# The first half of every expert placed alongside a 12-chunk recurrence, with the experts' weights in quarter slices

## The chip, the cores and the metric

One core of a Trainium2 chip. Its engines run side by side, each through its own list of instructions in order: PE (TensorE) does matmuls, in which one operand is loaded as weights and the other streams through; DVE (VectorE), ACT (ScalarE) and POOL (GpSimd) do elementwise work; SP only starts transfers, one after the other, and a transfer that has to wait holds up those behind it. The metric is the device time of one execution in microseconds (us), lower is better.

## What is computed

The reference, cut to what matters. A recurrence over 768 steps for 4 x 8 heads with a 40 x 40 state each, and then a mixture of eight experts of which every token takes one.

```python
for t in range(S):                                   # 768 steps, state (4, 8, 40, 40)
    y[:, :, t] = np.einsum('bhd,bhde->bhe', rt, state)
    Sa = np.einsum('bhde,bhe->bhd', state, at)
    state_decay = state * wt[:, :, None, :] - np.einsum('bhd,bhe->bhde', Sa, bt)
    state = state_decay + np.einsum('bhd,bhe->bhde', vt, kt)
...
logits = x @ w_gate                                  # x: the 3072 tokens of y, 320 wide
e_idx = np.argmax(logits, axis=1)
for e in range(E):                                   # 8 experts, w1 320 x 1024, w2 1024 x 320
    h = np.maximum(x[mask] @ w1[e], 0.0)
    out[mask] = gate_w[mask, None] * eom[mask, e, None] * (h @ w2[e])
```

All inputs and outputs are float32.

## The kernel before, in words

**The recurrence** (class `Att`) is cut into 12 chunks `c` of 64 steps, and each chunk into two halves of 8 head pairs, `q` = 0 and 1; I call one (c, q) a half chunk, and there are 24. A chunk needs three things. `prep` scales the inputs and builds small triangular matrices: matmuls `pl` (L241) and transposes `pt` (L159), with the running products of `scan` (L118). `tinv` inverts 32 x 32 triangles on DVE (L276 to L317, tiles `tmpf`, `Tt`, `Yt`), for a batch of two chunks at a time, and brings the result through DRAM into the tile `Tc` (L325, two buffers). `crit` is the serial part of a half chunk: a matmul into the PSUM tile `pa` (L370, two buffers), a solve (L380), a correction (L407), a second solve (L380), each with a copy by ACT in between, and the state of the next chunk by `pS` (L427) and two DVE operations (L432, L433). `tail` makes the output of the half chunk: transposes `ptU` and `ptS` (L449, L456), `pM` (L463), `pY` (L480, L481), and the DVE product `x` (L483), which is thus done once per half chunk. After most steps of `crit` and `tail` a few matmuls with zero weights are issued that compute nothing (`fill`, `warm`, L128, tile `fl`).

**The routing.** `route` writes `x` to DRAM, transposes it (`pxt`, L635) and computes its logits (L642). `pick` then ranks the tokens of a batch of chunks: matmuls of one-hot rows (L679 to L687), some twenty small DVE operations on the tile `mem`, and scatters into a table `tab` in DRAM (L714), in which each expert owns 480 slots. The batches (`NB`) come after chunks 3, 7, 10 and 11. After chunk 7 (`HALF`) the next free slot of every expert is moved to at least 240, so that the first two of its four tiles of 120 slots hold tokens of chunks 0 to 7 alone and can be worked on from then.

**The experts** (class `Moe`). A float32 number is split into a high part and a rest, and a product is the sum of three matmuls. `weights` loads all of an expert's w1 and w2 into staging tiles `st` (L738 to L748), lets ACT round a copy (`w1h`, `w2h`) and DVE subtract it (`w1l`, `w2l`, L744, L750). `tokens` gathers the rows of its tiles (`xg`, L764), transposes them (`px`, L772) and splits them (`xh`, `xl`, L774, L775). `expert` goes over eight blocks of 128 hidden units: eight matmuls into `ph` (L794, as many columns as there are slots: 240 for two tiles, 480 for four), of which the last has 64 rows of weights, then `hh` by ACT and `hl` by DVE (L798, L799). I call these eight a hidden block. Then, per tile of 120 slots, 24 matmuls into `po` (L807 to L809), a scaling (L811) and a scatter to the output (L812).

**The order of the work.** `run` (L500 on) interleaves by hand: after each step of `crit` a step of the previous `tail`, four steps (`RATE`) of a background list, and one of the routing. The background is `prep` and `tinv` of all chunks in turn, and then `early`: weights of expert 0, its first two tiles, and five (`E0`) of its hidden blocks. `need(c + 1)` runs the background until the inverses of the next chunk are emitted. When the chunks are done, `experts` does the rest, unit by unit: experts 0 and 1 in two halves, 2 to 7 with all four tiles. A scheduler of the language then sorts the list of each engine by its own estimate of time, so what stands in the lists is read below from the built programs.

Of the kernel before, what the change touches and what calls it, by code (L numbers as in the profile page):

```python
# [21 lines left out]
NP = 16  # L22
FAST = 1
DSC = 4
RATE = 4

# [27 lines left out]
class Att:  # L54
# [3 lines left out]
    def __init__(s, ctx, tc, ident, win, din, rl, vl, vt, nch=12):  # L58
# [23 lines left out]
        s.Tt = s.cp.tile([128, 1056], F32, name="Tt")  # L82
# [12 lines left out]
        s.fl = s.ps.tile([128, 512], F32, name="fl", tag="fl")  # L95
        s.buffers()
        s.st, s.ld, s.post, s.idle, s.NsOf = {}, {}, [], False, {}
# [32 lines left out]
    def fill(s, step, x):  # L130


        s.warm(x, s.FILL[step])
# [127 lines left out]
    def tinv(s, cs):  # L261
# [97 lines left out]
    def crit(s, c, q):  # L359
# [7 lines left out]
        pa = s.ps.tile([128, 8, 40], F32, name="pa", tag="pa", bufs=2)  # L367
# [130 lines left out]
    def run(s, sink, then=None):  # L498
# [5 lines left out]
        ready = {}  # L504

        def preps(b):
            for c in b:
                yield from s.prep(c)
                if c + 1 < n:
                    s.scan(c + 1)  # L510

        def inv(b):
            yield from s.tinv(b)
            for c in b:
                ready[c] = True
# [18 lines left out]
        def need(c):  # L534
            while c not in ready:
                next(bg)
        need(0)
# [11 lines left out]
        for c in range(n):  # L549
            need(min(c + 1, n - 1))  # L550
            for q in range(2):
                for i, _ in enumerate(s.crit(c, q)):
# [8 lines left out]
                    adv(RATE)  # L561
# [13 lines left out]
E0 = 5  # L575


class Moe:
    def __init__(s, ctx, tc, ident, wg, wo, w1, w2, out):
# [22 lines left out]
        nc.vector.tensor_scalar(out=s.bnd, in0=iw, scalar1=float(CAP), scalar2=float(TS * s.HT), op0=ALU.mult, op1=ALU.add)  # L602
# [21 lines left out]
    HALF, HT, half = 7, 2, False  # L624
    NB = {3: (0, 4), 7: (4, 4), 10: (8, 3), 11: (11, 1)}
# [101 lines left out]
    def weights(s, e, wp, sp):  # L727

        nc = s.nc
        w1h = wp.tile([128, 3, FF], F32R, name="w1h", tag="w1h")  # L730
        w1l = wp.tile([128, 2, FF], F32R, name="w1l", tag="w1l")
        w2h = wp.tile([128, 8, DM], F32R, name="w2h", tag="w2h")
        w2l = wp.tile([128, 8, DM], F32R, name="w2l", tag="w2l")
        yield w1h, w1l, w2h, w2l
        for k in range(3):
            st = sp.tile([128, FF], F32, name="st", tag="st")
            if k < 2:
                nc.sync.dma_start(out=st, in_=s.w1[e, 128 * k:128 * k + 128])  # L738
            else:
                for h in range(2):  # L740
                    nc.sync.dma_start(out=st[64 * h:64 * h + 64], in_=s.w1[e, 256:320])
            nc.scalar.copy(out=w1h[:, k], in_=st)
            l, r = (w1l[:, k], slice(0, 128)) if k < 2 else (w1h[64:128, 2], slice(64, 128))
            nc.vector.tensor_tensor(out=l, in0=st[r], in1=w1h[r, k].bitcast(F32), op=ALU.subtract)  # L744
            yield
        for k, n in ((0, 3), (3, 3), (6, 2)):
            st = sp.tile([128, FF], F32, name="st", tag="st")[:, 0:n * DM].rearrange("p (k f) -> p k f", k=n)
            nc.sync.dma_start(out=st, in_=s.w2[e, 128 * k:128 * (k + n)].rearrange("(k p) f -> p k f", p=128))  # L748
            nc.scalar.copy(out=w2h[:, k:k + n], in_=st)
            nc.vector.tensor_tensor(out=w2l[:, k:k + n], in0=st, in1=w2h[:, k:k + n].bitcast(F32), op=ALU.subtract)  # L750
            yield

    def tokens(s, tabs, e, t0, nt, pool, psx):

        nc = s.nc
        m = 2 if pool is s.tp0 else 4
        rows = 256 * (s.HALF + 1) if t0 + nt <= s.HT else NTOK
        xh = pool.tile([128, 3, TS * m], F32R, name="xh", tag="xh")[:, :, 0:TS * nt]
        xl = pool.tile([128, 3, TS * m], F32R, name="xl", tag="xl")[:, :, 0:TS * nt]
        xg = pool.tile([TS, m, DM], F32, name="xg", tag="xg")  # L760
        tb, ti = (x[:, :, 4 * e + t0:4 * e + t0 + nt] for x in tabs)
        yield tb, ti, xh, xl
        for t in range(nt):
            nc.gpsimd.indirect_dma_start(out=xg[:, t], out_offset=None, in_=s.xd[0:rows],  # L764
                                         in_offset=bass.IndirectOffsetOnAxis(ap=ti[:, 0, t:t + 1], axis=0),
                                         bounds_check=rows - 1, oob_is_err=True)
        yield
        for k in range(3):
            n = 128 if k < 2 else 64
            pt = psx(TS * nt)  # L770
            for t in range(nt):
                nc.tensor.transpose(out=pt[0:n, TS * t:TS * t + TS], in_=xg[:, t, 128 * k:128 * k + n],  # L772
                                    identity=s.ident[0:TS, 0:TS])
            nc.scalar.copy(out=xh[0:n, k], in_=pt[0:n])  # L774
            nc.vector.tensor_tensor(out=xl[0:n, k], in0=pt[0:n], in1=xh[0:n, k].bitcast(F32), op=ALU.subtract)  # L775
            if k == 2:
# [297 lines left out]
```

## Time and profile before

| what | us |
|---|---|
| median of 3 runs (lowest, highest) | 951.22 (943.26, 955.48) |
| the profiled execution: its own time | 950.18 |
| its span, which the profile covers | 948.5 |
| first `x` of the recurrence | 128.50 |
| `x` of half chunks 18 and 24 (the last) | 521.39 and 662.28 |
| last matmul of the experts | 932.79 |

In the profile a row of a timeline gives the start, the length, the engine, the line, the operation, output and inputs, and in brackets how long the engine had been idle and what ended the wait. The length of a matmul is modelled and overlaps that of the next, so what a matmul costs in a stream is read from the distance between two starts. PEclk is the granted clock of PE, 1.00 being full speed. A row of a windows table gives the busy time of every engine in a stretch, its PEclk, the busy share of the transfer engines and the bytes moved. In the profile's records a float32 matmul is two entries (`pM x8` is four matmuls); those of the experts are one entry each.

### The profile page before, as it was taken

How to read it: one execution, taken by the hardware profiler on the slowest of the kernel's cores; microseconds unless marked ns; L12 is line 12 of the kernel's file. 1: busy time of each engine (PE TensorE's matmuls, PEld its weight loads, DVE VectorE, ACT ScalarE, POOL GpSimd, SP SyncE). 2: the span in 40 equal slices, each digit the busy share in tenths (PEclk: the TensorE clock that was granted, in tenths of full speed). 3: DMA queues.
4: the chain of work that ended last, by engine and by line, in shares of the span. 5: the costliest groups of instructions: out<-in, count | busy, mean ns of one | idle time of the engine just before them, and what ended most of it. 6: DMA issues, size and time to landing. Idle time of an engine off the chain costs nothing.

```text
span 948.5 us, 22268 instructions
## 1 busy us (share of the span) xinstructions
PE 864.7 (91%) x9226; PEld 720.2 (76%) x9226; DVE 508.5 (54%) x1040; ACT 352.0 (37%) x835; POOL 324.4 (34%) x520
## 2 busy tenths in 40 slices
PE   6569699899999999999994999999899999999993
PEld 5457478788788788887873788888788788788873
DVE  8656948957944882388872321112535553544320
ACT  2566354754356135635211311111324542433110
POOL 7445567576255534502012000002252412231001
PEclk9555759999599669999876565556699999999997
DMA  8965277476266427535334321000655634351000
GB/s 187 187 124 116 60 164 157 99 178 136 74 145 131 100 77 177 109 81 125 80 81 73 86 49 35 24 24 13 162 146 157 180 116 119 87 162 55 11 14 23
DMA packets 151749, 97.77 MB, mean 103 GB/s; under 512 B 122678, under 2 KB 136825, under 8 KB 151642
## 3 DMA queue, kind: packets, MB, share of 16 engines
q1 hardware_dynamic: 146922, 87.30, 39.6%
q0 software_dynamic: 3840, 8.91, 3.3%
q8 instruction: 74, 1.21, 0.5%
q14 instruction: 33, 0.27, 0.1%
q10 hardware_dynamic: 880, 0.08, 0.1%
HBM read 73.48 MB, written 18.26 MB: 97 GB/s over the span
## 4 chain that ended last, share of the span: by engine, by line
PE 64%; DVE 14%; issue 8%; DMA 7%; POOL 3%; ACT 1%; SPq 0%; POOLq 0%; ACTq 0%; DVEq 0%
PE ph L794 14%; PE fl L128 7%; DVE tmpf L309 6%; PE pM L463 5%; PE po L809 5%; PE po L807 4%; PE po L808 4%; PE pa L380 3%; PE pl L241 3%; PE pa L370 2%; PE pS L427 2%; PE pY L481 2%; PE pxt L642 2%; PE pY L480 2%; DMA Nd<-N 2%
## 5 line engine op out<-in xcount | busy, mean ns | idle before, releaser
L247 POOL TENSOR_SCALAR_AFFINE_SELECT LA<-LA 64x192 f32<-64x192 f32 x144 | 62.4, 458 | 107.2 <-ACT LA L245 106.6
L714 POOL DMA_INDIRECT tab<-rec,si x24 | 25.1, 1045 | 211.7 <-DVE rec L711 174.3
L799 DVE SCALAR_TENSOR_TENSOR hl<-ph,hh 128x480 fp32r<-128x480 f32 (+1 forms) x75 | 41.8, 565 | 89.0 <-ACT hh L798 88.9
L794 PE MATMUL ph<-xl,w1h 128*128 128x480 f32 (+3 forms) x225 | 86.0, 383 | 0.0
L812 POOL DMA_INDIRECT out_dram<-y,ti x32 | 34.4, 1074 | 150.3 <-DVE y L811 90.3
L241 PE MATMUL pl<-Am,KBt 120*128 120x192 f32 (+1 forms) x288 | 71.7, 398 | 15.1 <-ACT Am L234 12.4
L794 PE MATMUL ph<-xh,w1h 128*128 128x480 f32 (+1 forms) x225 | 82.0, 366 | 0.6 <-DVE mem L692 0.3
L807 PE MATMUL po<-w2h,hh 128*120 128x320 f32 x256 | 80.2, 317 | 0.0
L808 PE MATMUL po<-w2l,hh 128*120 128x320 f32 x256 | 78.9, 312 | 0.0
L809 PE MATMUL po<-w2h,hl 128*120 128x320 f32 x256 | 78.4, 323 | 0.0
L798 ACT ACTIVATE hh<-ph 128x480 fp32r<-128x480 f32 (+1 forms) x75 | 36.6, 498 | 109.4 <-PE ph L794 109.4
L241 PEld LDWEIGHTS pl<-Am,KBt 120*128 120x128 f32 x288 | 57.0, 241 | 20.7 <-ACT Am L234 13.0
L463 PE MATMUL pM<-R,VU 104*128 104x128 f32 x384 | 71.4, 346 | 0.0
L118 POOL TENSOR_TENSOR Q<-Q,w 120x96 f32<-120x96 f32 x112 | 66.7, 634 | 0.1
L463 PEld LDWEIGHTS pM<-R,VU 104*128 104x128 f32 x384 | 61.7, 245 | 5.8 <-issue 2.3
L380 PE MATMUL pa<-As,Tc 32*32 32x40 f32 x1664 | 58.9, 224 | 6.2 <-ACT Tc L328 3.4
L469 DVE TENSOR_TENSOR M<-pM,mM 128x512 f32<-128x512 f32 x34 | 23.4, 689 | 74.6 <-PE pM L463 74.4
L481 PE MATMUL pY<-KB,M 128*64 128x40 f32 x768 | 62.1, 253 | 1.5 <-DVE M L469 1.2
L380 PEld LDWEIGHTS pa<-As,Tc 32*32 32x32 f32 x1664 | 46.7, 127 | 19.7 <-issue 7.0
L480 PE MATMUL pY<-Sd,R 104*64 104x40 f32 x704 | 60.2, 253 | 1.5 <-DVE M L469 1.5
L481 PEld LDWEIGHTS pY<-KB,M 128*64 128x64 f32 x768 | 54.5, 163 | 6.7 <-issue 4.0
L128 PE MATMUL fl<-As,zb 128*32 128x128 f32 x288 | 59.1, 338 | 0.0
(195 smaller groups left out, 1969.1 us busy)
## 6 DMA issues: line engine op xcount, KB each, us to landing
D<-in_din_dram SPq DMA_DIRECT2D x24, 540.0 KB
st<-in_w_dram SPq DMA_DIRECT2D x16, 512.0 KB
st<-in_w_dram SPq DMA_DIRECT2D x16, 480.0 KB
XS<-in_vt_dram SPq DMA_DIRECT2D x24, 256.0 KB
XU<-in_vt_dram SPq DMA_DIRECT2D x24, 256.0 KB
Nd<-N SPq DMA_DIRECT2D x24, 256.0 KB
VU<-in_vl_dram SPq DMA_DIRECT2D x24, 208.0 KB
w<-in_win_dram SPq DMA_DIRECT2D x12, 360.0 KB
```

The costliest lines, as they stand in the source:

```text
L118: g.tensor_tensor(out=run(m, z), in0=run(m - 1, z), in1=wr(m, z), op=ALU.mult)
L128: s.nc.tensor.matmul(s.fl[0:32, 0:src.free_size()], s.zb[0:src.partition_size()], src, start=True, stop=True)
L241: nc.tensor.matmul(pl[:, i, 0:nj], KBt[:, g0 + i].rearrange("p n t -> p (n t)"), Am[:, 0:nj, g0 + i], start=True, stop=True)
L247: g.affine_select(out=la[:, :, i], in_=la[:, :, i], pattern=[[0, nj], [1, C]], base=0, channel_multiplier=-1, compare_op=ALU.is_gt, fill=0.0)
L380: nc.tensor.matmul(pa[o:o + 32, i], Tc[o:o + 32, p, :], x[o:o + 32, i, :], start=True, stop=True, tile_position=(o, o))
L463: nc.tensor.matmul(pM[:, i], VU[:, h0 + i].rearrange("p n t -> p (n t)"), R[:, :, h0 + i], start=True, stop=True)
L480: nc.tensor.matmul(o, R[:, side, i, :], Sd[:, i, :], start=True, stop=False)
L481: nc.tensor.matmul(o, Ms[i // 4][:, i % 4, side, :], KB[:, side, p, :], start=not c, stop=True)
L794: nc.tensor.matmul(ph, l, r, start=(i == 0), stop=(i == 7))
L807: nc.tensor.matmul(po, hh[f][:, ts_], w2h[:, f], start=(f == 0), stop=False)
L808: nc.tensor.matmul(po, hh[f][:, ts_], w2l[:, f], start=False, stop=False)
L809: nc.tensor.matmul(po, hl[f][:, ts_], w2h[:, f], start=False, stop=(f == 7))
```

## The change

- All eight experts are split in two halves. `early` now holds the first two tiles of all of them (`E0 = 8`), `experts` the last two of all of them. Every expert's weights are thus loaded and split twice.
- The weights come in slices of 256 hidden units (`FS`): `load` brings one slice of w1 (three transfers) and of w2 (one), `split1` and `split2` make high part and rest. `walk` runs over slices and emits in turn a hidden block, then the second matmuls of the block before it for both tiles (`second`, six matmuls of 320 columns; I call it a second block), then half of the next slice's split. Slices are loaded two ahead in `early` (two raw buffers) and five ahead in `experts` (six).
- The last matmul of a hidden block now has all 128 rows: the rest of `xl` is set to zero (L795).
- `early` waits six background steps (`LATE`) between gathering the first tokens and transposing them. Sixteen of its steps on, `hush` ends all fills, and from there two background steps (`RATE2`) are taken per step of `crit`, not four.
- `HALF` is chunk 6, and the routing batches come after chunks 3, 6, 8, 9, 10 and 11.
- `crit` of a chunk asks for the chunk's own inverses and for the `prep` of the next, no longer for the inverses of the next; `Tc` has three buffers. `pa` has one buffer instead of two, and the bank of `fl` is shared with `po`, which `early` uses with two buffers. `Tt` moves to a pool that is freed after the last inverse.

The core of the diff (`slots` is only moved, `tokens` becomes `fetch` and `turn`, `expert` becomes `hidden` and `second`):

```diff
-            Tc = s.st[c]["Tc"] = s.p2.tile([128, NP, 32], F32, name="Tc")
+            Tc = s.st[c]["Tc"] = s.p2.tile([128, NP, 32], F32, name="Tc", bufs=3)
...
-        pa = s.ps.tile([128, 8, 40], F32, name="pa", tag="pa", bufs=2)
+        pa = s.ps.tile([128, 8, 40], F32, name="pa", tag="pa")
...
-            need(min(c + 1, n - 1))
+            need('t', c)
+            need('p', min(c + 1, n - 1))
...
-                    adv(RATE)
+                    adv(RATE2 if s.quiet else RATE)
...
-E0 = 5
+E0 = 8
+HT = 2
+FS = 256
+LATE = 6
...
-    HALF, HT, half = 7, 2, False
-    NB = {3: (0, 4), 7: (4, 4), 10: (8, 3), 11: (11, 1)}
+    HALF, half = 6, False
+    NB = {3: (0, 4), 6: (4, 3), 8: (7, 2), 9: (9, 1), 10: (10, 1), 11: (11, 1)}
...
+    def load(s, e, g, p):
+        fs = slice(FS * g, FS * g + FS)
+        r1 = p.tile([128, 3, FS], F32, name="r1", tag="r1")
+        r2 = p.tile([128, 2, DM], F32, name="r2", tag="r2")
+        nc.sync.dma_start(out=r1[:, 0:2], in_=s.w1[e, 0:256, fs].rearrange("(k p) f -> p k f", p=128))
+        for h in range(2):
+            nc.sync.dma_start(out=r1[64 * h:64 * h + 64, 2], in_=s.w1[e, 256:320, fs])
+        nc.sync.dma_start(out=r2, in_=s.w2[e, fs].rearrange("(k p) f -> p k f", p=128))
...
-            seq += [(w1h[:, 2, fs], xh[:, 2]), (w1h[0:64, 2, fs], xl[0:64, 2])]
+        seq += [(w1h[:, 2, fs], xh[:, 2]), (w1h[:, 2, fs], xl[:, 2])]
...
+    def walk(s, units, tabs, first, raw, ahead, wp, tp, hp, psx, ps1, ps2, m):
...
+        for k, u in enumerate(units):
...
+            for g in range(4):
+                i = 4 * k + g
+                if more and g == 0:
+                    xg = s.fetch(tabs, tp, m, *units[k + 1])
+                if more and g == 2:
+                    nt = s.turn(xg, units[k + 1][2], tp, m, psx)
+                    Tn = next(nt)
+                for fi in range(2):
+                    h = s.hidden(W[i], T, fi, hp, TS * m, ps1)
+                    yield
+                    if pend:
+                        s.second(*pend, hp, ps2)
+                        yield
+                    pend = W[i], u, tabs, 2 * g + fi, h
+                    if i + 1 < len(sl):
+                        split(i + 1, fi)
+                    next(nt, None)
+                load(i + 1 + ahead)
...
+        w = s.walk([(e, 0, 2) for e in range(E0)], tabs, W, raw, 2, wp, tp, hp, psx, psx, ps2, 2)
+        for _ in range(LATE + 10):
+            yield next(w)
+        quiet()
+        yield from w
...
+        units = [(e, 0, 4) for e in range(E0, E)]
+        for e in range(E0):
+            units.insert(2 * e + 1 if e < E - E0 else len(units), (e, HT, 2))
```

How it moves the lists of the engines is shown at two places. The first is PE in chunk 10, around the transposes `ptS` and the correction (`pa<-As2,NT`) of one half chunk. Before:

```order
L427 MATMUL pS_6979<-XU2_162,KB_4242 40x40 x8
L380 MATMUL pa_6992<-As_7011,Tc_4945 32x40 x13
L642 MATMUL pxt_6951<-G_70,xT_6955 128x16 x3
L380 MATMUL pa_6992<-As_7011,Tc_4945 32x40 x3
L128 MATMUL fl_146<-As_7011,zb_144 32x128 x2
L370 MATMUL pa_7193<-XS1_157,LA_4993 64x40
L456 MATMUL ptS_7045<-ident_58,XS2_161 128x40 x8
L128 MATMUL fl_146<-VU0_148,zb_144 32x128
L370 MATMUL pa_7193<-XS1_157,LA_4993 64x40 x4
L463 MATMUL pM_7055<-R0_147,VU0_148 128x128 x4
L407 MATMUL pa_6992<-As2_7043,NT_4245 32x40 x16
L128 MATMUL fl_146<-As2_7043,zb_144 32x128 x2
```

Now, at the same place:

```order
L461 MATMUL ptS_7510<-ident_58,XS2_161 128x40 x8
L412 MATMUL pa_7413<-As2_7508,NT_4780 32x40 x7
L468 MATMUL pM_7520<-R0_147,VU0_148 128x128 x4
L412 MATMUL pa_7413<-As2_7508,NT_4780 32x40 x9
L840 MATMUL po_7592<-w2h_7449,hh_7475 120x320
L841 MATMUL po_7592<-w2l_7450,hh_7475 120x320
L842 MATMUL po_7592<-w2h_7449,hl_7476 120x320
L840 MATMUL po_7593<-w2h_7449,hh_7475 120x320
L841 MATMUL po_7593<-w2l_7450,hh_7475 120x320
L468 MATMUL pM_7585<-R0_147,VU0_148 128x128 x4
L842 MATMUL po_7593<-w2h_7449,hl_7476 120x320
```

The fills are gone and a second block of an expert stands there. Before, the first matmul of the next half chunk (`pa_7193`) stood among the solves of this one (`pa_6992`); with one `pa` buffer it can't. In the list as a whole, 34 hidden blocks and 32 second blocks now stand ahead of the last `pY`, where there were five hidden blocks; 94 hidden and 96 second blocks stand behind it, where there were 75 hidden blocks (48 of 480 columns, 27 of 240) and 768 second matmuls, as many as 128 second blocks.

The second place is DVE where the early work begins, behind the last inverse (`Tt<-tmpf` 64x4x16). Before:

```order
L314 TENSOR_REDUCE Tt<-tmpf 64x4x16
L317 TENSOR_REDUCE Tt<-tmpf 64x4x16
L744 TENSOR_TENSOR w1l<-st,w1h 128x1024
L469 TENSOR_TENSOR M<-pM,mM 128x512
L432 TENSOR_TENSOR tmS<-XS_153,pS 40x320
L433 TENSOR_TENSOR XS_161<-tmS,Dt 40x8x40
```

Now, eight rows behind it:

```order
L429 TENSOR_TENSOR Dt<-LA 40x8
L766 TENSOR_TENSOR w1l<-r_6256,w1h 128x512
L767 TENSOR_TENSOR w1h<-r_6256,w1h 64x256
L775 TENSOR_TENSOR w2l<-r_6257,w2h 128x640
L766 TENSOR_TENSOR w1l<-r_6262,w1h 128x512
L767 TENSOR_TENSOR w1h<-r_6262,w1h 64x256
L678 TENSOR_REDUCE mem<-LG 128x4
L775 TENSOR_TENSOR w2l<-r_6263,w2h 128x640
L680 TENSOR_TENSOR mem<-LG,mem 128x4x8
L743 COPY tb<-tr 120x128
```

The splits of the first two slices, a routing batch (`mem`, that of chunk 8) and the copy of the slot table (`tb<-tr`) now stand in one piece, ahead of the next state update (`tmS`, `XS`).

More of the change, by code (lines that the diff above doesn't have):

```diff
@@ L25 @@
 RATE = 4
+RATE2 = 2
 def lay_inputs(r, k, v, w, a, b):
@@ L724, in overfull @@
         V.tensor_reduce(out=out, in_=t, axis=AX.X, op=ALU.max)
[L727 to L776, printed above, removed]
-                nc.scalar.copy(out=xh[64:128, k], in_=pt[0:64])
-            yield
@@ new lines, in hidden @@
+    def hidden(s, w, T, fi, hp, wd, ps1):
+        nc = s.nc
+        w1h, w1l = w[0:2]
+        xh, xl = T
+        n = xh.shape[-1]
+        fs = slice(128 * fi, 128 * fi + 128)
+        ph = ps1()[:, 0:n]
+        seq = []
+        for k in range(2):
+            seq += [(w1h[:, k, fs], xh[:, k]), (w1h[:, k, fs], xl[:, k]), (w1l[:, k, fs], xh[:, k])]
+        seq += [(w1h[:, 2, fs], xh[:, 2]), (w1h[:, 2, fs], xl[:, 2])]
+        for i, (l, r) in enumerate(seq):
+            nc.tensor.matmul(ph, l, r, start=(i == 0), stop=(i == 7))
+        a = hp.tile([128, wd], F32R, name="hh", tag="hh")[:, 0:n]
+        b = hp.tile([128, wd], F32R, name="hl", tag="hl")[:, 0:n]
+        nc.scalar.activation(out=a, in_=ph, func=AF.Relu)
+        nc.vector.scalar_tensor_tensor(out=b, in0=ph, scalar=0.0, in1=a.bitcast(F32), op0=ALU.max, op1=ALU.subtract)
+        return a, b
@@ new lines, in walk, with load, split @@
+    def walk(s, units, tabs, first, raw, ahead, wp, tp, hp, psx, ps1, ps2, m):
+        sl = [(u[0], g) for u in units for g in range(4)]
+        R, W = dict(enumerate(first)), {}
+        def load(i):
+            if i < len(sl) and i not in R:
+                R[i] = s.load(*sl[i], raw)
+        def split(i, h):
+            W[i] = W.get(i, ()) + (s.split2 if h else s.split1)(R[i][h], wp)
+            if h:
+                del R[i]
+        xg = s.fetch(tabs, tp, m, *units[0])
+        for i in range(ahead):
+            load(i)
+        split(0, 0)
+        split(0, 1)
+        load(ahead)
+        for _ in range(LATE):
+            yield
+        t = s.turn(xg, units[0][2], tp, m, psx)
+        T = next(t)
+        for _ in t:
+            yield
+        pend = None
+        for k, u in enumerate(units):
+            more = k + 1 < len(units)
+            nt = iter(())
+            for g in range(4):
[7 more added lines that the diff above has]
+                    h = s.hidden(W[i], T, fi, hp, TS * m, ps1)
+                    yield
+                    if pend:
+                        s.second(*pend, hp, ps2)
+                        yield
+                    pend = W[i], u, tabs, 2 * g + fi, h
[3 more added lines that the diff above has]
+                load(i + 1 + ahead)
+            for _ in nt:
+                yield
+            if more:
+                T = Tn
+        s.second(*pend, hp, ps2)
+        yield
@@ L835, in early @@
+    def early(s, ctx, psx, ps2, quiet):
+        pool = lambda n, b: ctx.enter_context(s.tc.tile_pool(name=n, bufs=b, side="right"))
+        raw, wp, tp, hp = pool("raw", 2), pool("wp", 2), pool("tp", 2), pool("hp", 4)
+        W = [s.load(0, g, raw) for g in range(2)]
         while not s.half:
             yield
-        s.tabs = s.slots(s.tp0)
-        t = s.tokens(s.tabs, 0, 0, 2, s.tp0, psx)
-        T = next(t)
-        yield from t
-        s.hp0 = ExitStack()
-        hp = s.hp0.enter_context(s.tc.tile_pool(name="hp0", bufs=E0, side="right"))
```

178 lines of the change are left out of this document (85 added, 93 removed).

## The prediction

> **What bounds the kernel now.** I read the page first (busy tenths, granted clock, chain), then the windows table by stages, then single rows where the price of one matmul was needed.
>
> ```profile
> PE   6569699899999999999994999999899999999993
> PEclk9555759999599669999876565556699999999997
> PE 64%; DVE 14%; issue 8%; DMA 7%; POOL 3%; ACT 1%; SPq 0%; POOLq 0%; ACTq 0%; DVEq 0%
> ```
>
> PE is busy nearly everywhere and leads the chain, but its clock is not full everywhere: late in the recurrence (slices 23 to 29) it is 0.5 to 0.6. The stages by windows:
>
> ```profile
> 358.00:466.00 108.00, 105.08 (x1794) 88.67 (x1792) 66.35 (x150) 51.84 (x134) 31.45 (x66) 1.00 0.53 121
> 521.39:662.77 141.38, 139.39 (x1504) 115.10 (x1502) 28.43 (x67) 25.89 (x68) 5.97 (x6) 0.56 0.14 38
> 562.50:648.00 85.50, 84.66 (x924) 69.59 (x923) 13.62 (x38) 13.12 (x35) 2.04 (x2) 0.50 0.08 24
> 662.77:933.14 270.37, 266.79 (x1471) 223.41 (x1471) 119.95 (x198) 90.66 (x158) 70.69 (x62) 0.97 0.38 107
> ```
>
> I call the stretch up to 521 us A, 521 to 663 B, the 270 us of experts behind it C. In B the background is used up, DVE and ACT are a fifth busy, and PE works without a gap at half speed: it is bound by a slow PE. C is bound by PE at full speed.
>
> What one half chunk costs on PE, with (first row) and without `prep`, and the fills' part of each:
>
> ```profile
> 384.28:403.16 18.88, 18.88 (x294) 15.90 (x291) 7.35 (x21) 13.77 (x35) 9.28 (x22) 1.00 0.59 125
> 575.78:603.14 27.36, 27.36 (x295) 22.37 (x294) 4.18 (x10) 3.83 (x10) 0.00 (x0) 0.50 0.11 31
> ...
> 384.28:403.16 18.88, 3.51 (x22) 1.91 (x22) 1.00 0.59 125
> 575.78:603.14 27.36, 6.96 (x26) 3.40 (x26) 0.50 0.11 31
> ```
>
> At half clock 27.36 - 6.96 = 20.4 us are the recurrence itself, so 10.2 us at full clock; the fills are 3.5.
>
> **The experts' prices.** Distances between starts at full clock, for a hidden block of 240 and of 480 columns, and for a second matmul:
>
> ```profile
> 690.16 0.27 PE L794 MATMUL ph<-xh,w1h 128*128 128x240 f32 x1
> 690.27 0.28 PE L794 MATMUL ph<-xl,w1h 128*128 128x240 f32 x1
> ...
> 691.03 0.37 PE L794 MATMUL ph<-xl,w1h 64*128 64x240 f32 x1
> 691.34 0.41 PE L809 MATMUL po<-w2h,hl 128*120 128x320 f32 x1
> ...
> 848.54 0.38 PE L794 MATMUL ph<-xh,w1h 128*128 128x480 f32 x1
> ...
> 850.57 0.48 PE L794 MATMUL ph<-xh,w1h 128*128 128x480 f32 x1
> ...
> 679.24 0.31 PE L809 MATMUL po<-w2h,hl 128*120 128x320 f32 x1
> 679.38 0.31 PE L807 MATMUL po<-w2h,hh 128*120 128x320 f32 x1
> ```
>
> A matmul of 240 columns takes 0.112 us, a block of eight would take 0.90, and takes 691.34 - 690.16 = 1.18: the one with 64 rows costs 0.28 more, ahead of it and behind. A block of 480 columns takes 2.03. The change gives that matmul all 128 rows, so I price its block at 0.90. A second matmul is 0.147, a block of six 0.88.
>
> **C, behind the last x.** The counts of before follow from these rows (three matmuls of this kind in each block), and the counts of after from its list, 94 hidden and 96 second blocks.
>
> ```profile
> L807 PE MATMUL po<-w2h,hh 128*120 128x320 f32 x256 | 80.2, 317 | 0.0
> L794 PE MATMUL ph<-xh,w1h 128*128 128x480 f32 x144 | 57.4, 398 | 0.0
> L794 PE MATMUL ph<-xh,w1h 128*128 128x240 f32 x81 | 24.6, 308 | 0.6 <-DVE mem L692 0.3 <-ACT xh L774 0.2
> ```
>
> Before: 48 x 2.03 + 27 x 1.18 + 768 x 0.147 = 242 us, and 7 for transposes: 249 of the 270; 21 are waits and a cold start. After: 94 x 0.90 + 96 x 0.88 + 5 = 174. It hides or not by DVE, which now splits every slice: 47 slices are left, each with these operations (512 columns 0.69 us and 256 columns 0.42, by the line through 640 and 960):
>
> ```profile
> L750 DVE TENSOR_TENSOR w2l<-st,w2h 128x960 fp32r<-128x960 f32 x16 | 18.2, 1157 | 9.3 <-ACT w2h L749 9.2
> L811 DVE TENSOR_SCALAR y<-po,tb 120x320 f32<-120x320 f32 x32 | 16.8, 546 | 43.4 <-PE po L809 43.4
> L799 DVE SCALAR_TENSOR_TENSOR hl<-ph,hh 128x240 fp32r<-128x240 f32 x27 | 11.0, 406 | 23.9 <-ACT hh L798 23.8
> L750 DVE TENSOR_TENSOR w2l<-st,w2h 128x640 fp32r<-128x640 f32 x8 | 6.6, 820 | 3.7 <-ACT w2h L749 3.6
> L775 DVE TENSOR_TENSOR xl<-px,xh 128x240 fp32r<-128x240 f32 x8 | 3.0, 402 | 1.9 <-ACT xh L774 1.9
> ```
>
> 0.69 + 0.42 + 0.82 + 2 x 0.41 + 0.30 + 0.27 = 3.3 us a slice, against 2 x (0.90 + 0.88) = 3.6 on PE. DVE is 90% full, and every wait for ACT in its list shows; so I keep the 21 us of waits, though the cold start goes. C becomes 195, a gain of 75. Bounds: 179 (5 us of waits) to 47 x 4.7 = 221, if in-order waits cost DVE 40%.
>
> The loads: a slice is 0.72 MB (the last 64 rows of w1 come twice), 34 MB in 195 us or 174 GB/s. The nearest rows:
>
> ```profile
> 0.00:50.00 50.00, 31.69 (x208) 27.60 (x209) 38.75 (x123) 20.14 (x57) 30.37 (x76) 0.77 0.92 188
> 670.00:680.00 10.00, 10.00 (x41) 8.90 (x41) 4.56 (x6) 4.15 (x6) 4.31 (x4) 0.57 0.97 270
> ```
>
> Large weight pieces reached 270 GB/s, the mixed small ones at the start 188; I take it that PE hides them, barely.
>
> The Trainium skill (DMA: Bandwidth & Descriptors, Bandwidth) speaks against this part: it wants transfers of 1 MiB and has 64 KB ones at 138 GB/s, 1 MB ones at 341. At 138 GB/s the 34 MB would be 246 us, and the sum 920. No run here shows 64 KB pieces alone.
>
> **B.** Ahead of the last `pY` stand 34 hidden and 32 second blocks with two dozen transposes: 61 us at full clock. The recurrence is five and a half half chunks of 10.2, 56 us; the fills go. So 117 us at full clock, 234 at half. Which? The clock held 1.00 for 108 us (358 to 466) where `prep` put some 5 us of large matmuls into each 18.9, and fell to 0.50 for good where only recurrence and fills were left (562 to 648), though PE had no gap there: it goes by how full the array is, not by whether PE is busy. Against me stands this:
>
> ```profile
> 540.00:550.00 10.00, 10.00 (x76) 8.03 (x77) 0.81 (x2) 1.75 (x5) 0.00 (x0) 0.50 0.27 49
> ```
>
> 24 of the old hidden matmuls did not lift the clock there. But those lost a quarter of their time to the 64-row one, and in B of after half of PE's time is dense, in every stretch of a few us. I take 0.88 with waits included, 133 us, a gain of 8; bounds 117 and 234.
>
> Where the clock changed earlier, one stretch at full and the next at half:
>
> ```profile
> 139.20:241.60 102.40, 97.43 (x1643) 82.03 (x1638) 80.45 (x159) 55.91 (x148) 68.35 (x114) 1.00 0.64 141
> 241.60:262.10 20.50, 20.38 (x216) 17.19 (x217) 19.95 (x32) 8.66 (x23) 6.60 (x9) 0.50 0.24 60
> ```
>
> The Trainium skill (TensorE: Matmul & The Clock Gate, Part 1) says that the clock follows PE's business in free-running windows of 3.4 us and falls in idle ones. The changes of the clock here do lie whole multiples of that apart (139.2 to 241.6, 241.6 to 262.1), but 562 to 648 shows half clock without idleness. By its rule alone B would be 117, and the sum 853.
>
> **A.** Its longer part, from the `x` of half chunk 3 to that of 17:
>
> ```profile
> 204.57:521.40 316.83, 293.12 (x4328) 245.78 (x4327) 206.02 (x428) 132.46 (x341) 120.09 (x210) 0.85 0.49 110
> ```
>
> That is 316.83 / 14, some 22 us a half chunk. The `prep` and `tinv` work is the same, and its list ends within a half chunk of where it did. `tinv` is asked for later, which may take DVE bursts off the state update; one `pa` means that a half chunk's first matmul waits for the last copy of the one before, and what PE does meanwhile is the `tail`, 10 us against a chain of about 7 (four groups of matmuls, by my estimate about 0.8 each, and five ACT steps by the row below, with their waits). I price both at 0, bounds -20 and +20. Two things at its end:
>
> ```profile
> L374 ACT COPY As<-pa 128x320 f32<-128x320 f32 x24 | 10.2, 426 | 43.3 <-PE pa L370 37.7 <-PE fl L128 4.8 <-PE pa L391 0.7
> ...
> 510.00:520.00 10.00, 0.39 (x2) 0.29 (x2) 0.47 (x2) 0.94 (x1) 2.22 (x2) 0.56 0.73 119
> ...
> PE px L772 <- DMA xg<-xd,ti: 12.6, 1, 12.6
> ```
>
> PE stood 12 us for the first gathered tokens, and `x`, the states and everything in PE's list behind the transposes with it. `LATE` and the earlier `HALF` shift that, but the gather now hangs behind the last inverse, two slices of splits and a routing batch on DVE, which the state update waits for too. I take 8 of the 12 to stay: -4, bounds -12 and +8. And two more routing batches:
>
> ```profile
> 664.40 1.57 PE L642 MATMUL pxt<-G,xT 128*128 128x16 f32 x6 [0.67 <-ACT xT L638]
> 667.28 0.19 PE L679 MATMUL pxt<-mem,tri 128*128 128x16 bf16 x1 [1.30 <-DVE mem L676]
> ```
>
> Each holds PE's list 1.3 us or more for DVE: +5 for two, with the two later waits.
>
> The startup's end and the 15.4 us behind the last matmul stay. **The sum**, from the profiled execution's 950.2 (span 948.5 and 1.7 around it; the median of the three runs is 951.2): 950.2 - 75 (C) - 8 (B) - 4 + 5 = 868, near 869 by the median. I say 869.
>
> **Rivals.**
> 1. DVE or the loads pace C (21 us of waits become 47 to 72): 895 to 920. For it: 90% on DVE, four transfers a slice. Against: DVE was half idle with the same operations, 270 GB/s seen. 0.16.
> 2. The clock stays between 0.52 and 0.6 in B, as in the whole of B before (0.56): 117 / 0.56 = 209 us, the sum 944, no change. 0.09.
> 3. Slower: half clock throughout B. Place: the solves of B, where PE waits for `pa`'s one buffer with no fill left; each gap of a microsecond or two lets the clock fall, and dense blocks at half speed then stand in front of the next solve. Price 234 - 133 = 101, sum 969; with A's half chunks going from about 22 to 27 us in a quarter of its 18 (another 20) 990. It decides from a mean clock of 0.50 in B on. Against: each solve now has dense blocks beside it. 0.08.
> 4. The lists don't do what the title says: half of the early blocks stand behind the recurrence anyway, so the experts are moved only in part. That is in the sum (94 of 128 remain); worse is that DVE's pile at the start of `early` delays it by one more half chunk, some 20 us less in B, 885. 0.10.
> 5. A gains as well (fewer drops of the clock to half between 241 and 358): 845. 0.07.
>
> The forecast has 0.50. Two per cent, 19 us, is about what a measurement of this kernel can tell from no change. Faster by more: 0.50 + 0.16 + 0.10 + 0.07 = 0.83; same 0.09; slower 0.08. The range goes from 832 (A -10, B 120, C 182) to 925, the end of the first rival.
>
> **What would show it.** Right: PEclk at 0.8 or more from the first early block to the last `x`; the last `x` near 650; some 195 us from there to the last matmul; hidden blocks 0.90 apart; no fills in B; DVE near 80% or more behind the recurrence. Wrong: PEclk at 0.5 to 0.6 in B (rivals 2, 3); PE idle in C behind splits or `r1`, `r2` loads (1); `x` of half chunk 18 far from 515 (A).

## The result, and the profile after

The changed kernel takes 885.33 us (median of 4 runs, 875.90 to 896.43); the kernel before, run beside it, 947.60 (943.26 to 955.48). The ratio is 0.930, with a 95% interval of 0.918 to 0.942: faster by 7%. I had said 869, between 832 and 925. The profiled execution took 882.89 us, with a span of 881.2. Executions of one and the same kernel on one chip differ by up to 6%, the slower ones with a lower granted clock of PE (0.78 to 0.84 among those of the kernel before), so ratios with an interval are of the fast executions of both kernels, and where these were too few I give medians over all.

The page's busy tenths of PE and its clock, to be laid beside those of before:

```profile
PE   6469799799999998999988979999999878999993
PEclk9755558896868699799788666999998999999997
```

The row of 0.5 and 0.6 late in the recurrence is nearly gone: of the 40 slices, only the 23rd to the 25th still have 0.6 there, and behind them the clock is 0.9 or more in all slices but two (0.8 and 0.7).

The stages, from the windows table of the changed kernel: A (up to the `x` of half chunk 18), B in two pieces, and C (last `x` to last matmul). The columns are length, busy us of PE, PEld, DVE, ACT and POOL, then PEclk, busy share of the transfers, GB/s.

```profile
0.00:516.01 516.01, 461.10 (x6191) 386.92 (x6192) 360.39 (x766) 233.90 (x608) 241.45 (x451) 0.77 0.55 118
516.01:546.00 29.99, 24.83 (x314) 21.77 (x311) 13.22 (x42) 9.27 (x23) 8.72 (x9) 0.61 0.75 172
546.00:664.80 118.80, 118.80 (x1584) 109.16 (x1583) 70.82 (x165) 56.88 (x130) 24.43 (x25) 1.00 0.50 141
664.80:867.35 202.55, 188.82 (x1400) 181.02 (x1399) 144.13 (x308) 110.19 (x234) 50.37 (x53) 0.97 0.67 186
```

| stage | before, us | predicted | after |
|---|---|---|---|
| A, to `x` of half chunk 18 | 521.4 | 522 | 516.0 |
| B, to the last `x` | 141 | 133 | 148 |
| C, to the last matmul | 270 | 195 | 202.5 |
| behind it, to the end of the span | 15.4 | 15.4 | 13.8 |

So the gain is C's, 68 us, and B is 7 us longer than before. By the prices of the prediction B now holds 61 us of experts' blocks and transposes, where it had five hidden blocks, for these 7 us.

The six half chunks of B, by the same table:

```profile
516.01:555.30 39.29, 34.13 (x404) 30.23 (x402) 17.82 (x51) 13.20 (x30) 10.90 (x10) 0.70 0.72 166
555.30:583.10 27.80, 27.80 (x313) 24.54 (x313) 15.95 (x32) 14.29 (x33) 4.55 (x5) 1.00 0.52 150
583.10:606.90 23.80, 23.80 (x351) 21.45 (x352) 15.80 (x45) 10.63 (x26) 7.55 (x7) 1.00 0.53 151
606.90:627.80 20.90, 20.90 (x335) 19.45 (x336) 11.82 (x24) 10.35 (x24) 2.54 (x3) 1.00 0.41 114
627.80:649.60 21.80, 21.80 (x322) 20.57 (x321) 11.89 (x36) 9.76 (x23) 4.04 (x4) 1.00 0.51 130
649.60:664.30 14.70, 14.70 (x173) 14.18 (x173) 10.29 (x21) 7.91 (x18) 3.56 (x4) 1.00 0.48 148
```

Five of them run at full clock without a gap. Half chunk 19 alone doesn't: 39.3 us, 5.2 of them idle, clock 0.70. Of B's 34 hidden and 32 second blocks it has 5 and 4. This is no chance of one execution: three more kernels with the same blocks there (`a_row64`, `a_E5`, `a_E7`, all below) took 46, 41 and 41 us for it, and in all seven profiles of kernels with such blocks in B, half chunks 21 to 24 ran at a clock of 1.00. What PE waited for in it:

```profile
PE pa L385 <- ACT As L416: 2.6, 1, 2.6
PE pa L412 <- ACT As L408: 1.9, 1, 1.9
```

And ACT's list at that place:

```profile
519.68 0.83 ACT L765 CAST w1h<-r 128x768 fp32r<-128x768 f32 x1 [1.24 <-DMA r<-in_w_dram]
520.41 0.72 ACT L774 CAST w2h<-r 128x640 fp32r<-128x640 f32 x1
521.04 0.42 ACT L408 COPY As<-pa 128x320 f32<-128x320 f32 x1
522.46 0.83 ACT L765 CAST w1h<-r 128x768 fp32r<-128x768 f32 x1 [1.01 <-DMA r<-in_w_dram]
...
523.81 0.72 ACT L774 CAST w2h<-r 128x640 fp32r<-128x640 f32 x1 [0.45 <-DMA r<-in_w_dram]
524.44 0.42 ACT L416 COPY As<-pa 128x320 f32<-128x320 f32 x1
```

The two copies of the solve stand behind the rounding of the first two slices, which in turn waited for their loads. The solve's matmuls wait for the copies, and nothing else is ready for PE: the fills have ended and the first hidden block starts at 540.45 by the timeline.

In C, the hidden block has its new price, 715.08 - 714.18 = 0.90:

```profile
714.18 0.27 PE L822 MATMUL px<-xh,w1h 128*128 128x240 f32 x1
...
714.97 0.27 PE L822 MATMUL px<-xl,w1h 128*128 128x240 f32 x1
715.08 0.31 PE L840 MATMUL po<-w2h,hh 128*120 128x320 f32 x1
```

and these are its largest waits:

```profile
PE px L801 <- DVE xl L804: 4.6, 2, 2.4
PE po L840 <- DVE y L846: 2.5, 1, 2.5
PE po L840 <- ACT hh L825: 2.2, 3, 1.8
```

PE is idle for 202.6 - 188.8 = 13.7 us there, all but 0.1 of it ahead of 760, where the early blocks end and the late ones begin; I call this the seam. At the seam the loads are dense, with the transfer engines fully busy, and ACT, whose rounded copies DVE's splits wait for, waits for them in turn (the second row is of 664.8 to 760):

```profile
680.00:700.00 20.00, 16.74 (x126) 15.14 (x124) 16.12 (x46) 12.50 (x25) 7.01 (x8) 1.00 1.01 273
...
ACT w1h L765 <- DMA r<-in_w_dram: 12.6, 7, 3.2
```

Behind 760 there is no gap:

```profile
760.00:867.35 107.35, 107.22 (x837) 105.16 (x835) 83.95 (x170) 63.31 (x136) 28.41 (x30) 1.00 0.60 173
```

### The profile page after: what moved, and what is told of

Read it like the earlier page. It is cut to its first block, busy times and chain, and to the rows that moved or that the text cites. A ratio compares the mean times of both kernels' runs of the same rounds, so it can differ in the third digit from the quotient of the medians.

```text
span 881.2 us, 23781 instructions
## 1 busy us (share of the span) xinstructions
PE 794.0 (90%) x9478; PEld 699.0 (79%) x9478; DVE 589.7 (67%) x1283; ACT 410.2 (47%) x994; POOL 327.0 (37%) x539
## 5 line engine op out<-in xcount | busy, mean ns | idle before, releaser
L785 POOL DMA_INDIRECT xg<-xd,ti x32 | 37.8, 1181 | 104.3 <-PE px L801 80.7
L775 DVE TENSOR_TENSOR w2l<-r,w2h 128x640 fp32r<-128x640 f32 x64 | 52.8, 824 | 21.9 <-ACT w2h L774 20.8
L842 PE MATMUL po<-w2h,hl 128*120 128x320 f32 x256 | 64.1, 317 | 0.6 <-DVE hl L826 0.5
L765 ACT CAST w1h<-r 128x768 fp32r<-128x768 f32 x64 | 53.0, 828 | 14.9 <-DMA r<-in_w_dram 14.8
L774 ACT CAST w2h<-r 128x640 fp32r<-128x640 f32 x64 | 46.5, 727 | 28.3 <-PE po L842 22.8
L485 PEld LDWEIGHTS pY<-Sd,R 104*64 104x64 f32 x704 | 50.4, 158 | 11.7 <-DVE M L474 6.6
L766 DVE TENSOR_TENSOR w1l<-r,w1h 128x512 fp32r<-128x512 f32 x64 | 44.1, 689 | 22.0 <-ACT w1h L765 21.1
L314 DVE TENSOR_TENSOR tmpf<-Tt,Yt 128x512 f32<-128x512 f32 (+5 forms) x62 | 58.3, 973 | 0.5
L822 PE MATMUL px<-xh,w1h 128*128 128x240 f32 x192 | 57.2, 299 | 1.4 <-DVE hl L826 0.9
L385 PE MATMUL pa<-As,Tc 32*32 32x40 f32 x1664 | 51.4, 217 | 5.7 <-ACT As L416 3.2
```

What stands on the lines that cost most here:

```text
L314: V.tensor_tensor(out=tm, in0=in0, in1=in1, op=ALU.mult)
L485: nc.tensor.matmul(o, R[:, side, i, :], Sd[:, i, :], start=True, stop=False)
L765: nc.scalar.copy(out=h, in_=r)
L822: nc.tensor.matmul(ph, l, r, start=(i == 0), stop=(i == 7))
L842: nc.tensor.matmul(po, b[:, ts_], w2h[:, f % 2], start=False, stop=(f == 7))
```

## The experiments

Each is timed against the kernel before on the same chip. The first two separate one small edit of the change, the 128 rows of the last matmul of a hidden block, from the rest of it.

**The kernel before with 128 rows** (`b_row128`).

```diff
+        nc.gpsimd.memset(xl[64:128, 2].bitcast(F32), 0.0)
...
-            seq += [(w1h[:, 2, fs], xh[:, 2]), (w1h[0:64, 2, fs], xl[0:64, 2])]
+            seq += [(w1h[:, 2, fs], xh[:, 2]), (w1h[:, 2, fs], xl[:, 2])]
```

> The kernel before, with one edit: the last matmul of a hidden block uses all 128 rows, the rest of xl being zero. Theory 1 (the matmul with 64 rows costs 0.27 us of the stream ahead of it and behind it, as the rows of 240 and of 480 columns show): 80 blocks lose 0.27 each, 22 us in all, so a ratio of 0.977 to the kernel before, some 926 us; a hidden block of 480 columns takes 1.76 instead of 2.03. Rival (the pause belongs to the end of the block, not to the 64 rows): block and time stay, ratio 1.00.

Measured: 932.4 us median (912.7 to 959.8) against 957.3 (933.6 to 986.3), a ratio of 0.974. Two starts in a stream of hidden matmuls of 480 columns, eight matmuls apart:

```profile
803.30 0.38 PE L795 MATMUL ph<-xh,w1h 128*128 128x480 f32 x1
...
805.04 0.39 PE L795 MATMUL ph<-xh,w1l 128*128 128x480 f32 x1
```

The eight take 1.74 us, 2.03 before: theory 1 holds in the block, and the median agrees with it. In the profiled execution (912.7 us) C is 255 us instead of 270, and B 111 instead of 141. B is that short because the clock was full in half chunks 20 and 21 and then fell again, with the same 13 fills in each; whether the edit had a part in that isn't shown. Half chunks 21 and 22:

```profile
570.60:586.30 15.70, 15.70 (x297) 13.22 (x295) 4.17 (x9) 3.84 (x10) 0.00 (x0) 1.00 0.20 54
586.30:607.90 21.60, 21.60 (x298) 18.11 (x295) 3.84 (x8) 3.84 (x10) 0.00 (x0) 0.69 0.09 27
```

**The changed kernel with 64 rows** (`a_row64`), the same edit the other way round.

> The changed kernel, with the last matmul of a hidden block back at 64 rows. Theory 1: 128 blocks pay 0.27 us again, 35 us, of which those in the recurrence (34) may also lose the full clock: 920 us if the clock holds from 546 us on, 940 to 960 if it falls to 0.5 for a good part of the recurrence's last stretch. Rival (PE has slack in the experts because DVE or the loads set the pace there): less than 15 us, below 900.

Measured: 919.3 us median (903.5 to 931.7), a ratio to the kernel before of 0.974 (0.953 to 0.995), where the change has 0.930. The pause is back, 0.20 or 0.31 from start to start around the matmuls with 64 rows instead of 0.11:

```profile
783.78 0.27 PE L822 MATMUL ph<-xh,w1h 128*128 128x240 f32 x1
783.98 0.38 PE L822 MATMUL ph<-xl,w1h 64*128 64x240 f32 x1
784.29 0.38 PE L822 MATMUL ph<-xh,w1h 128*128 128x240 f32 x1
784.60 0.37 PE L822 MATMUL ph<-xl,w1h 64*128 64x240 f32 x1
```

```profile
494.30:660.40 166.10, 157.88 (x1888) 137.93 (x1885) 84.60 (x207) 66.36 (x152) 33.62 (x35) 0.89 0.50 134
660.40:888.00 227.60, 219.42 (x1400) 190.57 (x1399) 145.36 (x308) 112.75 (x234) 51.88 (x53) 0.98 0.60 166
```

C is 25 us longer, which is 94 blocks by 0.27: PE sets C's pace, not DVE or the loads. The clock in B held (0.89), so matmuls with 64 rows don't keep it down; what I had argued from the 24 old hidden matmuls was wrong in that, and why they did not lift the clock stays open.

**What lifts the clock.** Three kernels take the kernel before and add fills behind the last inverse, which compute nothing: 14 more in one burst with 128 output columns of weights (`b_wide`), the same burst with 32 (`b_narrow`), and twice as many everywhere without a burst, 32 columns (`b_spread`).

```diff
# b_wide: w = 128 behind the last inverse; b_narrow: w = 32
-            s.nc.tensor.matmul(s.fl[0:32, ...], s.zb[0:src.partition_size()], src, ...)
+            s.nc.tensor.matmul(s.fl[0:w, ...], s.zb[0:src.partition_size(), 0:w], src, ...)
...
-        s.warm(x, s.FILL[step])
+        s.warm(x, s.FILL[step] + (14 if s.idle and step == 's0' else 0))
# b_spread instead
+        s.warm(x, s.FILL[step] * (2 if s.idle else 1))
```

> The kernel before; once the last inverse is in the list, the fills have 128 output columns of zero weights instead of 32, and 14 more of them stand behind the first solve of each half chunk. They compute nothing. Theory A (the clock goes by how full the array is): the burst lifts the clock to 1.0 and most of the stretch behind half chunk 18 runs at 0.8 or more; a half chunk there takes some 10.2 us of recurrence and 27 fills of 0.27, 17 to 19 us instead of 27; total 895 to 920. Theory B (the clock goes by PE being busy, or falls in this stretch for another reason than density): the clock stays near 0.5, a half chunk takes 35 us, total 985 to 1000.

> The control of the one with wide fills: the same number of fills at the same places, all with 32 output columns as before. Theory A (density): the clock stays near 0.5 behind half chunk 18, five half chunks take 14 x 0.53 us = 7.4 us more each, and some of it ahead of them, total 985 to 1000. Theory B (PE being busy decides): the same time as with wide fills, whatever that is.

> The kernel before; once the last inverse is in the list every step issues twice as many fills (26 in a half chunk instead of 13, all with 32 output columns), with no burst. Theory C (a stretch of gapless wide matmuls as long as a window of the clock lifts it; the same matmuls spread among the small ones don't): the clock stays near 0.5 behind half chunk 18, a half chunk there takes 27.4 + 13 x 0.5 = 34 us, the stretch from half chunk 18 to the last x some 165 us, the kernel 3% slower or more. Rival (the amount of wide matmuls decides, wherever they stand): a half chunk takes 18 to 20 us as it did with 14 of them in one burst, clock 0.87 or more.

Measured: 947.2 us (ratio 1.002, 0.994 to 1.010), 954.4 against a median before of 957.3, and 945.0 (0.989, 0.974 to 1.004). Half chunk 21 or 22 of each, in this order:

```profile
628.90:647.40 18.50, 18.50 (x329) 17.10 (x327) 3.83 (x7) 3.83 (x10) 0.00 (x0) 1.00 0.12 31
```

```profile
596.00:614.60 18.60, 18.60 (x322) 15.96 (x320) 4.16 (x9) 3.83 (x10) 0.00 (x0) 1.00 0.18 46
```

```profile
610.90:629.10 18.20, 18.20 (x329) 15.67 (x327) 3.86 (x8) 3.83 (x10) 0.00 (x0) 1.00 0.11 32
```

All three have a clock of 1.00 there, and a half chunk with twice the fills takes 18 us where it took 27. Of the theories only a part is left. How many of the array's columns a matmul uses plays no part that can be seen (A expected the narrow burst to fail), and a burst isn't needed (C expected the spread fills to fail). With 26 or 27 fills the clock was 0.92 to 1.00 in half chunks 20 to 22 of all three. With 13 it is not fixed: 0.50 in half chunks 21 and 22 of the kernel before, 1.00 in half chunks 20 and 21 of `b_row128` and then 0.69 and 0.59. PE shows no gap in any of these, so "PE busy" doesn't tell them apart. What it is in the fills that lifts the clock isn't shown. The share of time in which long streams run would fit these rows, but not the one of 540 to 550 in the prediction, where 24 hidden matmuls of 240 columns, 0.21 us from start to start, took half of the time at a clock of 0.50.

These kernels win little or nothing overall: the fills begin ahead of half chunk 18, whose `x` came at 549.8, 533.5 and 534.4 instead of 521.4. (In `b_row128`, without more fills, it came at 529.1, so not all of that need be the fills'.)

**Both small edits together** (`b_cheap`): 128 rows, and twice the fills, on the kernel before.

> The kernel before with two small edits and nothing moved: 128 rows in the last matmul of a hidden block (0.977 expected of it alone), and twice as many fills behind the last inverse (0.989 measured for it alone). Theory 1 (two separate gains, blocks and clock): the product, 0.965, some 920 us, the half chunks behind number 19 at a clock of 0.95 or more in 18 us. Theory 2 (the blocks with 128 rows already lift the clock, so the fills add only their own time): 0.975 to 0.985.

Measured: 917.9 us (908.6 to 930.0), ratio 0.962 (0.956 to 0.967): theory 1, by the time. Its half chunk 22:

```profile
616.70:634.90 18.20, 18.20 (x329) 15.67 (x327) 3.84 (x8) 3.84 (x10) 0.00 (x0) 1.00 0.11 32
```

Nothing is moved here and no expert beyond the two of before is cut in two, and it has 0.038 of the change's 0.070. The profile shows where this comes from for the rows alone: that execution took 930.0 us, C was 249 us instead of 270, and the last `x` came at 664, about as in the kernel before (662), since half chunk 18 came 20 us later. The fills' part is seen in the ratio only.

**The fills kept** (`a_fills`).

```diff
-        if not s.quiet:
-            s.warm(x, s.FILL[step])
+        s.warm(x, s.FILL[step])
```

> The changed kernel with the fills kept to the end of the recurrence (everything else, the two background steps included, as changed). Theory (PE has no gap there, so each of some 13 fills in each of six half chunks is paid): 78 x 0.21 to 0.27 us, 16 to 21 us longer between half chunk 18 and the last x, a ratio of 1.02 to the changed kernel (0.95 to the one before). Rival (the first 30 us of that stretch are slow because the clock has fallen, and fills lift it): no longer, or up to 10 us shorter.

Measured: 902.2 us, ratio 0.944 (0.931 to 0.958). The ratio is near the 0.95 of the theory, though its interval overlaps that of the change (0.918 to 0.942), and the time is not lost in the place that the theory says: with the fills in its estimate the scheduler leaves only 8 hidden and 8 second blocks ahead of the last `pY`, and B is short, at a clock of 0.87:

```profile
507.90:626.40 118.50, 111.56 (x1646) 95.24 (x1644) 42.87 (x125) 35.14 (x88) 17.61 (x17) 0.87 0.34 88
```

So this run doesn't price the fills alone. It shows that 26 hidden and 24 second blocks less, 45 us by their prices, with 64 fills in their place make B only 30 us shorter. At 0.21 us a fill (14 more made the half chunk of `b_narrow` 2.9 us longer than that of `b_row128`) the 64 are 13 us, which is nearly the difference.

**The inverses emitted as early as before** (`a_tinv`).

```diff
-            need('t', c)
+            need('t', min(c + 1, n - 1))
```

> The changed kernel, with the inverses of the next chunk asked for as before the change (the three buffers stay). The list then has 44 hidden blocks ahead of the last pY, not 34. Theory 1 (PE is full on both sides, so work moved ahead is paid where it goes): the experts' stretch becomes 18 us shorter, the recurrence as much longer, time within 10 us of the changed kernel. Theory 2 (the later inverses take DVE bursts off the state update): also 10 to 20 us slower up to half chunk 18. Theory 3 (there is idle time and half clock between half chunks 16 and 19 to be filled): 10 to 20 us faster than the changed kernel.

Measured: 903.4 us, ratio 0.941 (0.929 to 0.954). C is shorter, by 23 us (179 us for 84 hidden and 85 second blocks), about what was moved. In the profiled execution, which took 912.2 us, the `x` of half chunk 18 comes at 556 instead of 516, and DVE is busy for 39.6 of the last 59.4 us of that with the inverses above all, while PE stands for 10:

```profile
496.80:556.20 59.40, 48.97 (x745) 43.07 (x745) 39.61 (x73) 14.24 (x35) 10.81 (x11) 0.65 0.56 121
716.90:896.00 179.10, 168.15 (x1251) 161.97 (x1252) 129.33 (x279) 97.37 (x210) 44.74 (x47) 0.96 0.65 187
```

That looks like theory 2, but the same three half chunks, 16 to 18, are no different in the change:

```profile
457.83:516.01 58.18, 54.61 (x821) 46.36 (x820) 39.37 (x77) 12.85 (x33) 8.00 (x9) 0.74 0.34 76
```

The 40 us are lost ahead of them, little by little from half chunk 4 to 15, in an execution with a mean clock of 0.73 there instead of 0.77. The intervals of the two ratios overlap too. So theory 2 is not shown; theory 3 (a gain) is not borne out.

**Fewer early experts**, five (`a_E5`) and seven (`a_E7`).

```diff
-E0 = 8
+E0 = 5
```

> The changed kernel with five early experts instead of eight: the last three run with all four tiles at once, so that 12 slices fewer are loaded and split behind the recurrence (35 instead of 47). The PE work behind the last x is the same by the prices (46 x 0.90 + 24 x 1.76 + 96 x 0.88 + 4 = 172 us instead of 174), the recurrence's list too. Theory 1 (the 28 us of waits behind the last x come from loads and splits): 10 to 15 us faster than the changed kernel, 870 to 875. Theory 2 (they come from the change from one stage to the other and from the in-order lists): within 5 us of it.

> The changed kernel with seven early experts instead of eight: 22 hidden blocks of 240 columns are left behind the last x, then one expert with four tiles. Theory 1 (the waits behind the last x come from loads and splits, and the 18.6 us wait for gathered tokens that came with five early experts comes back only where too few early blocks are left to cover the routing): 22 blocks with their second blocks are 39 us of cover, no wait for tokens over 3 us, 4 slices fewer to split, 3 to 6 us faster than the changed kernel, ratio to the one before 0.925. Rival (the cover is already too short): a wait of 5 us or more for the gathered tokens, no gain.

Measured: 886.9 us, ratio 0.932 (0.921 to 0.943), and 882.9 us, ratio 0.912 (0.906 to 0.918). PE's largest waits in C, first with five, then with seven:

```profile
PE px L801 <- DMA xg<-xd,ti: 21.2, 4, 18.6
PE po L842 <- DVE hl L826: 2.2, 2, 1.1
```

```profile
PE po L840 <- DVE y L846: 4.4, 1, 4.4
PE px L801 <- DVE y L846: 4.3, 1, 4.3
```

With five, the last routing has only six early blocks to hide behind, and PE stands 18.6 us for the gathered tokens of the first late unit. With eight, 30 early blocks are left, and PE never waits for tokens. The 13.7 us of idle time in the change are thus not the routing's; they are waits for DVE and ACT, and with 12 slices less to load and split they fell to 6 (27.3 us of idle time less the 21.2 for tokens). That agrees with theory 1 of `a_E5` for these 8 us, and the wait for tokens takes more than that back. With seven the wait for tokens is gone, and two of 4.4 and 4.3 us are there behind DVE's list; C was 206 us, no shorter. That profile is of an execution of 883.5 us, though, and the ratio of 0.912 comes from three of 868 to 874, so it can't say where a gain would be. Whether seven are faster than eight is open, but there is more for it than the two ratios taken on different chips: `a_pool` and `a_best` below were run beside each other and differ in the number of early experts alone, eight and seven, and have 0.934 (0.929 to 0.938) and 0.920 (0.914 to 0.927); by the medians over all of their executions, 888.8 and 884.0, the difference is 0.5%.

**The first rounding copies on POOL** (`a_pool`), and together with seven early experts (`a_best`).

```diff
-        nc.scalar.copy(out=h, in_=r)
+        cp(out=h, in_=r)        # gpsimd.tensor_copy for the first two early slices
```

> The changed kernel with the rounding copies of the first two early slices done by POOL instead of ACT. Theory 1 (in half chunk 19 the copies of the solve stand in ACT's list behind these four, two of which wait for their loads: 2.3 and 2.1 us of PE's idle time): PE's waits for As there fall from 4.6 us to under 1, half chunk 19 from 39.3 to 34 us or less, the kernel 4 to 8 us faster, which is near what its times can tell. Rival (half chunk 19 is slow because the clock has fallen and its few wide matmuls don't lift it): the waits go, the half chunk keeps 37 us or more.

> The changed kernel with both: seven early experts, and the first two slices' rounding copies by POOL. If both theories hold their gains add up, 8 to 12 us: a ratio to the kernel before of 0.92 or below, some 875 us. If neither does: 0.93.

Measured: 888.8 us, ratio 0.934 (0.929 to 0.938), and 884.0 us, ratio 0.920 (0.914 to 0.927). Waits and half chunks 19 to 21 of the first:

```profile
PE pxt L689 <- DVE mem L686: 4.4, 1, 4.4
PE pa L385 <- ACT As L416: 0.6, 1, 0.6
```

```profile
507.30:536.70 29.40, 24.29 (x346) 21.29 (x345) 14.45 (x42) 6.02 (x17) 12.13 (x12) 0.61 0.79 177
536.70:568.10 31.40, 31.40 (x324) 27.39 (x324) 14.91 (x29) 14.05 (x32) 5.88 (x7) 0.93 0.43 118
568.10:600.20 32.10, 32.10 (x394) 28.18 (x393) 20.76 (x57) 14.81 (x34) 8.06 (x9) 1.00 0.63 164
```

The waits for `As` went from 4.5 us to 0.6, so ACT's list was their cause. In their place PE now waits 4.4 us for DVE's routing, and is idle for 5.1 us of half chunk 19 as it was for 5.2. Half chunk 19 is 10 us shorter, but it holds less than one block instead of nine; these stand in the next two half chunks and are paid there, and the six together take 151 us, 148 before. The local gain is given back within 64 us. `a_best` has the ratio that both theories together gave (0.92), but with a median of 884 and not their 875; as `a_pool` alone gains nothing, what `a_best` has beside the change would be the seven experts'.

## Why the prediction was right, and where it was off

**C** (195 forecast, 202.5): right in kind and nearly in size. The 75 us by which its list shrinks came: the blocks have the prices 0.90 and 0.88, and `a_row64` shows that each 0.27 us in a block is 0.27 us of the time. The 21 us that I kept beside the blocks are 28 now, but I had misread them. They were not waits: PE was idle for 270.37 - 266.79 = 3.6 us in C of before, and the rest was busy time that my prices miss, half clock at the start of C among it. Now 13.7 of the 28 are idle time and some 15 such busy time. So the waits did grow, by 10 us. The first rival, DVE's pace or the loads', is not true of C as a whole (its second half runs without a gap with DVE 78% busy), but has a part at the seam: there PE waits for DVE and ACT, ACT for the loads, and `a_E5`, with 12 slices less, has 6 us of these waits instead of 13.7. How much of it is the loads' and how much DVE's was not separated. The page of the Trainium skill by whose price for 64 KB transfers the sum would have been 920 (DMA: Bandwidth & Descriptors, Bandwidth) does not decide here: of the loads in C half are of that size by count, and the traffic was 186 GB/s on average, above the 174 that I had asked of it.

**B** (133 forecast, 148) is the term that was mis-sized. That the clock is full beside dense blocks was right: 1.00 from 546 us to the last `x`, where 0.50 had been. For half chunks 20 to 24 the step is right in size as well: 29 hidden and 28 second blocks, 51 us, and four and a half half chunks of 10.2 with transposes are 99, by 0.88 some 112; measured 109. The whole miss is half chunk 19: by my prices 5 hidden and 4 second blocks and 10.2 us, 22 with waits, and it took 39.3. I had let the dense blocks begin with B. They begin 25 us later, behind splits, gather and transposes, and until then PE works at a clock of 0.61 and waits 4.5 us for ACT's copies. I take it that the clock is low there because the fills have just been ended and the blocks haven't begun; that is not shown, since before, with its fills, this half chunk had a clock of 0.55, and with the fills kept (`a_fills`) 0.78 beside fewer blocks. That half chunks 20 to 24 came out to within 3 us is luck in part, for two errors cancel inside the sum. A half chunk's own work doesn't halve at full clock: at 1.00 it took 18.6 us with 27 fills (`b_narrow`) and 15.7 with 13 (`b_row128`), so a fill costs 0.2 and the rest 13, not 10.2. DVE and ACT are busy for the same 4.2 and 3.8 us in a half chunk at either clock; whether PE's list is held up by them isn't shown, as PE shows no gap. The 0.88 that I took for waits covered this, though in these five half chunks there are none.

**A** (+1 forecast, -5): not to be told from nothing. Up to half chunk 18 the change, `a_row64` and `a_E5` give PE the same work, and they reached it at 516.0, 494.3 and 507.5 us, with mean clocks of 0.77, 0.82 and 0.80. The 12.6 us wait for the first tokens is gone, and half chunk 19 has its successor, in ACT's list rather than DVE's, where I had put it. What the later routing, one `pa` and the later inverses did each was not separated.

**The rivals.** The second (clock 0.52 to 0.6 in B) and the third (slower) fell with the clock row. The fourth (early blocks later than they should be) is the one that came true in part: the first blocks came 25 us into B, which cost 15 us of the 20 that I had put there. The fifth (A gains as well) can't be told from the spread of A above.

**On the clock** I said that it goes by how full the array is and not by whether PE is busy. The runs with fills bear out the second half, as far as the profile's busy row shows it, and speak against the first: fills with 32 and with 128 columns of weights went with the same clock. What it goes by stays open. The Trainium skill (TensorE: Matmul & The Clock Gate, Part 1) has a free-running window and lets activity lift the clock. That the same list meets the clock differently in each execution (A above) agrees with the first; for the second PE's busy row is no measure, since it shows no gap at 0.50 and at 1.00.

**What the gain is made of.** By the separate and the undone edit, the 128 rows are worth 2.6% on the kernel before (0.974) and some 4% on the changed one (0.930 against 0.974, the latter with a wide interval). More fills in B give 0.989 alone, with an interval that reaches 1.004, so that share isn't clear. Both together, without moving anything, give 0.962 (0.956 to 0.967). The rest, some 3% of the 7, is what the experts' move earns beyond them: blocks that count stand where fills stood. By the prices, the rows make up 20 of the 75 us by which C's list shrinks and the moved blocks 54; B at its higher clock takes these in for 7 us.

## What to carry to other kernels

Where PE works without a gap and yet at half clock, look for small matmuls in its list: here, long ones among them, even ones that compute nothing, went with a full clock and a half chunk of 18 us instead of 27, and useful ones bring work along that has to be done anyway. Before moving work into such a stretch, price the cheap edits in the same rows (a pause of 0.27 us on a matmul with fewer rows, in every block), for here they have half the gain. And when work starts in the middle of a serial chain, its first copies stand in that chain's queues: look at half a chunk there row by row, since removing one wait only brought the next.

## What was not expected of the hardware

- A matmul with 64 rows of weights between ones of 128 rows costs 0.1 us more ahead of it and 0.2 behind it (0.20 and 0.31 from start to start instead of 0.11 at 240 columns, 0.27 in all for a block); with the missing rows zero and all 128 used, nothing (0.11).
- Beside fills with zero weights the clock was as full with 32 output columns as with 128: a half chunk of 18.6 and 18.5 us, both at 1.00.
- Half chunks with the same 13 fills ran at 0.50 for 85 us in the kernel before, where PE had 0.8 us of gaps in all, and two in a row at 1.00 in `b_row128`.
- At twice the clock the recurrence's half chunk, with 13 fills, takes 15.7 us instead of 27.4: a factor of 1.74, not 2.
- The same work of PE up to half chunk 18 took 516.0 us in one execution and 494.3 in another (the change and `a_row64`), with mean clocks of 0.77 and 0.82.
